# Pooled attention and a gelu MLP: another order at the start of the first product, and partial sums of group 0 kept in SBUF

## The chip, the cores and the metric

One core of a Trainium2 chip. The metric is the device time of one execution in microseconds (us); the median of 5 runs of the kernel before is 302.25 (302.09 to 302.32).

## What is computed

Attention with pooled keys and values, 8 batches of 8 heads, 576 queries, head size 64; then a two-layer MLP on its output as 4608 rows of 512:

```
k_p = k.reshape(B, H, 72, 8, D).mean(axis=3)          # 8 keys pooled into one; v the same
scores = q @ k_p^T / sqrt(D);  attn = softmax(scores)
x = (attn @ v_p) as (4608, 512)
h = x @ w_in                                          # 512 -> 2048
out = (0.5 * h * (1 + tanh(c * (h + 0.044715 h^3)))) @ w_out   # 2048 -> 512
```

## The kernel before

The work is one stream written out by hand in program order: each engine does its instructions in the order in which the code emits them, and waits come from the data. TensorE (PE) does all products, ScalarE (ACT) exponentials, logarithms and gelu, VectorE (DVE) the pooling, the multiplication by the inverse denominator and the eviction of results, GpSimd (POOL) issues most loads, SyncE (SP) the stores and the transposing DMAs.

**Batch 0** is done alone at the start (lines 425 to 481). Scores `qk` and `expo` for the halves c = 0, 1 of the queries and the pairs of heads pr = 0 to 3; `den0(c, pr, bank)` forms the denominators of two pairs at once, `inverse0` (L354 and L356 in the profile) their inverse as exp(-ln), `av0(c, pr, bank)` (L363) the weighted values, and `mult0` (L367) multiplies into xT, the transposed input of the MLP. `spin(n, bank)` (L421) is n matmuls of zeros whose result nobody reads. The values come through `v_steps(0)`, three adds on DVE (L150).

**Nine groups of 512 rows** follow, g = 0 to 8. Each has

- a first product, `p1_mm(g, fo, ko)` (L396): for each of 16 tiles fo of 128 hidden columns, four matmuls ko over the 512 inputs into the PSUM bank that `h_bank` names; ko is also the pair of heads that xT's rows come from, so ko 0 and 1 need `mult0` of pairs 0 and 1 only. `gelu` (L402) then writes gT.
- a second product, `p2_mm(g, r, fo, bank)` (L405): for each row tile r of 128 rows, 16 matmuls over fo into the bank that `o_bank` names (row tiles 0 and 2 share one bank, 1 and 3 the other); `store` evicts it on DVE (L410) and SP sends four DMAs (L415). The 64 matmuls are counted by m, and the attention of the next batch is hung in between by `at(m, f, ...)`.

Group 0's first product takes its first four tiles as ko 0, 1, and then ko 2, 3. During it DVE pools the keys of batch 1 (`k_steps`, L150) for the transposes `trans_k` after fo = 11 (L212). In its second product, `v_half(1, 0)` at m = 3 and `v_half(1, 1)` at m = 18 pool the values of batch 1, three DVE adds each, and the eight pieces of attention of batch 1 run at

```
pos = (6, 14, 20, 27, 34, 41, 48, 55, 61)
at(pos[i], qk, nb, *ORDER[i], 2)
a = (nb, *ORDER[i - 1], 4 + 2 * ((i - 1) % 2))
at(pos[i], av, *a)                      # bank 4 or 6, used by every second piece
at(min(pos[i] + 9, ...), mult, *a)      # DVE, L340
```

so `av` at m = 27 writes the bank that `mult` of m = 23 reads. Its second product takes rows 0 and 1 together, four fo at a time, then row 2, then row 3. Batch 2 and later use another way: the keys go through kz and a transposing DMA on SP to kx (L178), which `rem_scores` at m = 2 of the group before (L296) reads. Their loads are issued by `load_next`, held back for batch 2 by a copy `gate` on POOL (L506) until q of batch 2 has been transposed by DMA (L256).

**Loads.** q of batch 0, w_in (two halves along the input), k, part of v and q of batch 1, w_out (four quarters along the hidden size), and q of batch 2 are issued by POOL in this order on one queue; a DMA on it waits for the eighth before it. The first k and v come through SP and ACT; v of batch 1 (`load_v(1, [nc.sync])`) through SP, released by a one-column memset of its tile on DVE (L485).

Of the kernel before, what the change touches and what calls it, by code (L numbers as in the profile page):

```python
# [8 lines left out]
F32 = mybir.dt.float32  # L9
BF16 = mybir.dt.bfloat16  # L10
ALU = mybir.AluOpType
# [7 lines left out]
def kernel(  # L19
# [9 lines left out]
    nc = tc.nc  # L29
# [3 lines left out]
    DM = H * D  # L33
    DF = moe_w_in.shape[1]
    KO = DM // 128
    FO = DF // 128
    T = S // 32
    TP = T // 2
    CH = S // 2
# [11 lines left out]
    ep = ctx.enter_context(tc.tile_pool(name="ep", bufs=2))  # L51
    gpool = ctx.enter_context(tc.tile_pool(name="gp", bufs=1))
    opool = ctx.enter_context(tc.tile_pool(name="op", bufs=5))
# [4 lines left out]
    PS = psp.tile([128, 8, 512], F32, name="PS")  # L58
# [4 lines left out]
    vts = [consts.tile([128, 4, 512], F32, name=f"vt{i}") for i in range(2)]  # L63
# [23 lines left out]
    def load_v(b, engs):  # L87
        rows = v[b].rearrange("h (j l) d -> j h (l d)", l=8)
        for i in range(2):
            engs[i % len(engs)].dma_start(out=vts[b % 2][64 * i:64 * i + 64], in_=rows[0:64, 4 * i:4 * i + 4])  # L90
# [8 lines left out]
    w_in_b = [consts.tile([128, KO // 2, DF], BF16, name=f"w_in_b{i}") for i in range(2)]  # L99

    w_out_b = consts.tile([128, FO, DM], BF16, name="w_out_b")
    w_in_v = moe_w_in.rearrange("(ko p) f -> p ko f", p=128)
# [8 lines left out]
    make_identity(nc, identb)  # L111

    def load_w_in(i):
        nc.gpsimd.dma_start(out=w_in_b[i], in_=w_in_v[:, 2 * i:2 * i + 2])  # L114

    load_w_in(0)
    load_w_in(1)
    load_k(1, [nc.gpsimd])
    load_q(1)
# [157 lines left out]
    def window(w, h):  # L277

        c = h * 2 * D - h % 2 * D
        return w.rearrange("j h a d -> j (h a d)")[:, c:c + 128]  # L280
# [63 lines left out]
    def den0(c, pr, bank):  # L344
        for x in range(2):
            e = es[0, c, pr + x]
            for y in range(2):
                one = ones.rearrange("j a d -> j (a d)")[:, 64 - 64 * y:192 - 64 * y]
                nc.tensor.matmul(out=PS[:, bank + x, :CH], lhsT=one, rhs=e[:, y, :],
                                 start=(y == 0), stop=(y == 1))  # L350

    def inverse0(c, pr, bank):
        ld = ep.tile([128, 2, CH], F32, name="ld0", bufs=1)
        nc.scalar.activation(out=ld, in_=PS[:, bank:bank + 2, :CH], func=ACT.Ln)  # L354
        rc = ep.tile([128, 2, CH], F32, name="rc0")
        nc.scalar.activation(out=rc, in_=ld, func=ACT.Exp, scale=-1.0)  # L356
        rcs[0, c, pr] = rc

    def av0(c, pr, bank):
        for x in range(2):  # L360
            e = es.pop((0, c, pr + x))
            for y in range(2):
                nc.tensor.matmul(out=PS[:, bank + x, :CH], lhsT=window(vz, 2 * (pr + x) + y),  # L363
                                 rhs=e[:, y, :], start=(y == 0), stop=(y == 1))

    def mult0(c, pr, bank):
        nc.vector.tensor_tensor(out=xT[:, pr:pr + 2, c * CH:(c + 1) * CH], in0=PS[:, bank:bank + 2, :CH],  # L367
                                in1=rcs.pop((0, c, pr)), op=ALU.mult)
# [7 lines left out]
    def x_bank(g):  # L376
        return g % 2

    def h_bank(g, fo):
        x, y = x_bank(g), 1 - x_bank(g)  # L380
        if g == 0 and fo < 4:
            return 4 + fo
        if g and fo == 4:
            return 5
        return (x, 2, 3, y)[fo if fo < 4 else (fo - 1) % 4]

    def o_bank(g, r):
        return 1 - x_bank(g) if r % 2 == 0 else x_bank(g)

    gTs = {}  # L390

    def p1_mm(g, fo, ko):
        r0 = g * GROUP
        q, j = divmod(fo, 4)
        w = w_in_b[ko // 2][:, ko % 2, q * 512 + j:(q + 1) * 512:4]
        nc.tensor.matmul(out=PS[:, h_bank(g, fo), :], lhsT=w, rhs=xT[:, ko, r0:r0 + GROUP],  # L396
                         start=(ko == 0), stop=(ko == KO - 1))

    def gelu(g, fo):
        if g not in gTs:  # L400
            gTs[g] = gpool.tile([128, FO, GROUP], BF16, name="gT")
        nc.scalar.activation(out=gTs[g][:, fo, :], in_=PS[:, h_bank(g, fo), :], func=ACT.Gelu_apprx_tanh)  # L402

    def p2_mm(g, r, fo, bank, c0=0, c1=DM):
        nc.tensor.matmul(out=PS[:, bank, c0:c1], lhsT=gTs[g][:, fo, r * 128:(r + 1) * 128],  # L405
                         rhs=w_out_b[:, fo, c0:c1], start=(fo == 0), stop=(fo == FO - 1))

    def store(g, r, bank):
        osb = opool.tile([128, DM], F32, name="osb")
        nc.vector.tensor_copy(out=osb, in_=PS[:, bank])  # L410

        for n in range(4):
            b, col = divmod(g * GROUP + r * 128 + n * 32, S)
            rows = out[b * S:(b + 1) * S].rearrange("(p t e) d -> e t p d", t=TP, e=2)
            nc.sync.dma_start(out=rows[col // CH, col % CH // 32], in_=osb[n * 32:(n + 1) * 32])  # L415


    def spin(n, bank):

        for _ in range(n):  # L420
            nc.tensor.matmul(out=PS[:, bank, :], lhsT=idle[:, 0:128], rhs=idle, start=True, stop=True)  # L421
# [24 lines left out]
    for h in range(H):  # L446
        nc.tensor.matmul(out=PS[64:Sp, 7, h * D:(h + 1) * D], lhsT=identb[0:64, h:64:H],
                         rhs=kps[0][0:64, KR], start=True, stop=True)
    scores(1, 1, 0)
    den0(0, 0, 2)  # L450
    inverse0(0, 0, 2)
    nc.vector.tensor_copy(out=vz[64:Sp, :, 0], in_=PS[64:Sp, 7].rearrange("p (h d) -> p h d", d=D))
    trans_q(0, *QG[2], 5, nc.vector)
# [8 lines left out]
    for f in v_steps(0):  # L462
        f()
    inverse0(1, 0, 6)
    spin(2, 4)
    den0(0, 2, 2)
    inverse0(0, 2, 2)
    spin(2, 4)
    av0(0, 0, 4)
    mult0(0, 0, 4)  # L470
    den0(1, 2, 6)
    inverse0(1, 2, 6)
    av0(1, 0, 0)
    mult0(1, 0, 0)
    av0(0, 2, 4)
    mult0(0, 2, 4)
    spin(2, 0)
    av0(1, 2, 0)
    mult0(1, 2, 0)
    for t in kps:  # L480
        nc.vector.memset(t[:, KR + 1], 0.0)
    nc.vector.memset(kTs[1][0], 0.0)
    nc.vector.memset(kTs[1][1], 0.0)

    nc.vector.memset(vts[1][:, 0, 0:1], 0.0)  # L485
    load_v(1, [nc.sync])
    for w in vps:
        nc.vector.memset(w, 8.0)
    nc.gpsimd.memset(kz, 0.0)

    for fo, ko in [(fo, ko) for ko in range(2) for fo in range(4)]:
        p1_mm(0, fo, ko)


    for g in range(NG):
# [41 lines left out]
        if g + 1 == NG:  # L537
# [3 lines left out]
            for i, o in enumerate(gLs):  # L541
                side[4 * i + 3].append(lambda i=i, o=o: nc.vector.tensor_copy(  # L542
                    out=o.rearrange("p f (x t) -> p f t x", t=4),
                    in_=gTs[g][:, 4 * i:4 * i + 4, 384:].rearrange("p f (t x) -> p f t x", t=4)))
# [1 line left out]


        if g == 0:
            first = [(fo, ko) for ko in (2, 3) for fo in range(4)]
        else:  # L550
            late = 3
            rest = [fo for fo in range(4) if fo != late]
            first = [(fo, ko) for ko in range(3) for fo in rest]
            first += [(fo, ko) for fo in (late, 4) for ko in range(3)]
            first += [(fo, 3) for fo in rest + [late, 4]]
        for fo, ko in first:
            p1_mm(g, fo, ko)
        for fo in range(FO):
            if fo >= (5 if g else 4):
                for ko in range(KO):  # L560
                    p1_mm(g, fo, ko)
            gelu(g, fo)
            for s in side[fo]:
                s()
# [2 lines left out]
            load_next()  # L567


        todo = {}  # L570

        def at(m, f, *a):
            todo.setdefault(m, []).append((f, a))
# [41 lines left out]
        seq = [(r, fo) for r in range(4 if g + 1 < NG else 3) for fo in range(FO)]  # L615
        if g == 0:

            seq[:32] = [(r, 4 * f4 + f) for f4 in range(4) for r in range(2) for f in range(4)]
        for m, (r, fo) in enumerate(seq):
            for f, a in todo.pop(m, []):  # L620
                f(*a)
            p2_mm(g, r, fo, o_bank(g, r))
            if fo == FO - 1:
                store(g, r, o_bank(g, r))
        for m in sorted(todo):
            for f, a in todo[m]:
                f(*a)
    for c0, c1, bank in ((0, 384, o_bank(g, 3)), (384, DM, 4)):
        for fo in range(FO):
            nc.tensor.matmul(out=PS[:, bank, c0:c1], lhsT=gLs[fo // 4][:, fo % 4], rhs=w_out_b[:, fo, c0:c1],  # L630
                             start=(fo == 0), stop=(fo == FO - 1))
        osb = opool.tile([128, c1 - c0], F32, name="osb")
# [35 lines left out]
```

## Time and profile before

| | us |
|---|---|
| median of 5 runs | 302.25 |
| the profiled execution: its time | 302.49 |
| its span | 300.4 |
| PE busy | 291.5 (97%) |
| ACT busy | 216.6 (72%) |
| DVE busy | 152.8 (51%) |
| first product of group 0 starts | 21.30 |
| second product of group 0 starts | 36.43 |
| first product of group 1 starts | 54.67 |

Times are from the start of the span. In lines of a timeline the columns are start, length, engine, line of the kernel, operation, output<-input, shape and count; in brackets the idle time of the engine before it and what ended that. PEld is the loading of weights, which goes on beside matmuls. Neighbouring instructions of a kind are merged, and some matmul records are missing from a trace. A matmul of 128x512 is reported with 379 ns, but such matmuls start 0.2157 us apart.

### The profile page before, as it was taken

What the parts mean: (1) busy time and instruction counts of PE and PEld (TensorE: products, weight loads), DVE (VectorE), ACT (ScalarE), POOL (GpSimd) and SP (SyncE); (2) the same over time, 40 slices, a digit from 0 to 9 for tenths busy, and PEclk for the clock granted to TensorE, in tenths of its full rate; (3) what the DMA queues carried; (4) which work ended last, traced back from release to release, by engine and by line L of the source; (5) the groups of instructions that cost most, each with busy time, mean ns of one, the idle gap of its engine ahead of it and who ended that gap; (6) DMA issues with size and microseconds to landing.
All of it is one profiled execution on the core that took longest, in us unless ns stands there. A gap on an engine that the chain in (4) does not pass through costs nothing.

```text
span 300.4 us, 4347 instructions
## 1 busy us (share of the span) xinstructions
PE 291.5 (97%) x1498; PEld 151.0 (50%) x1527; DVE 152.8 (51%) x303; ACT 216.6 (72%) x408; POOL 37.4 (12%) x67
## 2 busy tenths in 40 slices
PE   8889999999999999999999999999999999999995
PEld 3555555554555455545554555455545555445443
DVE  4775587474576257716690659065924630111112
ACT  1686679879888897889878987798879887206500
POOL 7104001300600060006000410032000000000000
PEclk9999999999999999999999999999999999999999
DMA  7999986980799169835994498729961310121022
GB/s 227 270 252 262 251 168 131 241 196 13 177 262 185 33 160 249 178 74 130 237 208 85 97 258 201 103 54 255 232 119 36 75 37 0 37 70 36 0 69 73
DMA packets 38758, 43.11 MB, mean 144 GB/s; under 512 B 25488, under 2 KB 26128, under 8 KB 38608
## 3 DMA queue, kind: packets, MB, share of 16 engines
q0 software_dynamic: 8000, 24.39, 36.0%
q1 hardware_dynamic: 30032, 17.06, 25.2%
q10 hardware_dynamic: 704, 1.38, 1.3%
q8 instruction: 12, 0.20, 0.3%
q14 instruction: 10, 0.08, 0.1%
HBM read 36.70 MB, written 9.44 MB: 154 GB/s over the span
## 4 chain that ended last, share of the span: by engine, by line
PE 87%; DMA 7%; POOL 1%; DVE 1%; issue 1%; ACTq 0%; ACT 0%; DVEq 0%; POOLq 0%
PE PS L405 40%; PE PS L396 38%; DMA kt<-in_v_dram 7%; PE PS L322 4%; PE PS L311 2%; PE PS L630 1%; DVE kt L150 1%; PE PS L296 1%; PE PS L287 1%; PE PS L267 1%; POOL w_in_b L114 0%; POOL qb L95 0%; PE PS L236 0%; ACTq L183 0%; ACT gT L402 0%
## 5 line engine op out<-in xcount | busy, mean ns | idle before, releaser
L405 PE MATMUL PS<-w_out_b,gT 128*128 128x512 bf16 x543 | 134.5, 379 | 0.9 <-issue 0.2
L396 PE MATMUL PS<-xT,w_in_b 128*128 128x512 bf16 x565 | 125.7, 379 | 0.7
L402 ACT ACTIVATE gT<-PS 128x512 bf16<-128x512 f32 x144 | 79.2, 606 | 45.7 <-PE PS L396 45.7
L396 PEld LDWEIGHTS <-w_in_b 128*128 128x128 bf16 x576 | 65.0, 113 | 58.8 <-DMA w_in_b<-in_moe_w_in_dram 0.3
L405 PEld LDWEIGHTS <-gT 128*128 128x128 bf16 x560 | 53.8, 97 | 51.0 <-issue 1.7
L340 DVE TENSOR_TENSOR xT<-PS,rc 64x288 bf16<-64x288 f32 x112 | 51.0, 455 | 20.4 <-ACT rc L332 17.8
L410 DVE COPY osb<-PS 128x512 f32<-128x512 f32 x35 | 24.2, 692 | 50.2 <-PE PS L405 46.8
L317 ACT ACTIVATE eT<-PS 64x576 bf16<-64x576 f32 x48 | 30.7, 640 | 0.6
L304 DVE COPY eT<-er 8x576 bf16<-8x576 bf16 x24 | 7.3, 303 | 39.3 <-ACT er L302 38.8
L329 ACT ACTIVATE ld<-PS 64x288 f32<-64x288 f32 x56 | 22.5, 403 | 5.6 <-PE PS L322 5.1
L332 ACT ACTIVATE rc<-ld 128x288 f32<-128x288 f32 x56 | 24.8, 443 | 1.8
L373 ACT ACT_TABLE_LOAD x17 | 21.8, 1283 | 3.6 <-issue 3.3
L150 DVE TENSOR_TENSOR kt<-kt 128x1280 f32<-128x1280 f32 (+5 forms) x18 | 18.9, 1048 | 10.2 <-DMA kt<-in_v_dram 6.5
L330 ACT ACTIVATE ld<-PS 64x288 f32<-64x288 f32 x56 | 22.5, 403 | 1.4
L322 PE MATMUL PS<-eT,vp 72*128 72x288 bf16 x96 | 19.7, 285 | 0.1
L150 DVE TENSOR_TENSOR vt<-vt 128x1024 f32<-128x1024 f32 (+3 forms) x18 | 17.1, 952 | 1.8 <-DMA vt<-in_v_dram 1.5
L502 POOL COPY gate<-eT 1x2 bf16<-1x2 bf16 x5 | 0.9, 174 | 125.3 <-DMA eT<-er 125.3
L322 PEld LDWEIGHTS <-vp 72*128 72x128 bf16 x96 | 9.5, 98 | 11.3
L274 ACT ACTIVATE e<-PS 72x576 bf16<-72x576 f32 x16 | 9.9, 644 | 2.9 <-PE PS L267 2.6
L421 PE MATMUL PS<-idle 128*128 128x512 bf16 x32 | 9.5, 434 | 1.6 <-DVE idle L139 1.2
L311 PE MATMUL PS<-qT,kx 128*128 128x288 bf16 x48 | 9.8, 286 | 0.0
L542 DVE COPY kt<-gT 128x512 bf16<-128x512 bf16 x4 | 3.0, 745 | 11.6 <-ACT gT L402 11.6
(64 smaller groups left out, 128.4 us busy)
## 6 DMA issues: line engine op xcount, KB each, us to landing
out_dram<-osb SPq DMA_DIRECT2D x141, 64.0 KB
kt<-in_k_dram POOLq DMA_DIRECT2D x12, 512.0 KB, 6.8
vt<-in_v_dram POOLq DMA_DIRECT2D x12, 512.0 KB, 10.5
qb<-in_q_dram POOLq DMA_DIRECT2D x7, 576.0 KB, 14.9
w_in_b<-in_moe_w_in_dram POOLq DMA_DIRECT2D x2, 1024.0 KB, 16.7
w_out_b<-in_moe_w_out_dram POOLq DMA_DIRECT2D x4, 512.0 KB, 24.4
vt<-in_v_dram SPq DMA_DIRECT2D x3, 512.0 KB
kt<-in_k_dram POOLq DMA_DIRECT2D x1, 1024.0 KB, 22.4
```

The lines of the kernel that those rows point to most:

```text
L150: nc.vector.tensor_tensor(out=o, in0=a, in1=b, op=ALU.add)
L317: nc.scalar.activation(out=eT[0:64, 2 * pr:2 * pr + 2, c, :], in_=PS[64 * c:64 * c + 64, 2:4, :CH], func=ACT.Exp, scale=1.0 / 64.0)
L322: nc.tensor.matmul(out=PS[:, bank + x, :CH], lhsT=window(vps[b % 2], 2 * pr + x), rhs=eT[:, 2 * pr + x, c, :], start=True, stop=True)
L329: nc.scalar.activation(out=ld[0:64], in_=PS[64:128, bank, :CH], func=ACT.Ln)
L330: nc.scalar.activation(out=ld[64:128], in_=PS[0:64, bank + 1, :CH], func=ACT.Ln)
L332: nc.scalar.activation(out=rc, in_=ld, func=ACT.Exp, scale=-1.0)
L340: nc.vector.tensor_tensor(out=xT[rows, pr, col:col + CH], in0=PS[rows, bank + x, :CH], in1=rc[rows], op=ALU.mult)
L373: nc.scalar.preload_act_table_set(name)
L396: nc.tensor.matmul(out=PS[:, h_bank(g, fo), :], lhsT=w, rhs=xT[:, ko, r0:r0 + GROUP], start=(ko == 0), stop=(ko == KO - 1))
L402: nc.scalar.activation(out=gTs[g][:, fo, :], in_=PS[:, h_bank(g, fo), :], func=ACT.Gelu_apprx_tanh)
L405: nc.tensor.matmul(out=PS[:, bank, c0:c1], lhsT=gTs[g][:, fo, r * 128:(r + 1) * 128], rhs=w_out_b[:, fo, c0:c1], start=(fo == 0), stop=(fo ...
L410: nc.vector.tensor_copy(out=osb, in_=PS[:, bank])
```

## The change

- `load_w_in`: the first half of w_in comes as two DMAs, hidden columns 0 to 1023 and 1024 to 2047, so nine DMAs instead of eight stand ahead of w_out.
- Batch 0: `av0(1, 0)` goes ahead of `den0(1, 2)`, `av0(1, 2)` ahead of `av0(0, 2)` and into bank 2; the last filler `spin(2, 0)` is gone; rc0 has three buffers.
- The memset that releases `load_v(1)`, and that load, come ahead of the other memsets.
- First product of group 0: six tiles on ko 0 and 1, then the same six on ko 2 and 3, each tile's two matmuls together; other banks.
- Second product of group 0: all four row tiles on fo 0 to 7 (rows 0 and 1, then 2 and 3), then on fo 8 to 15 (rows 2 and 3, then 0 and 1). Rows 0 and 1 are copied to SBUF after fo = 7 (m = 11 and 15), and their second half is added to that copy in `store`.

```diff
     def load_w_in(i):
-        nc.gpsimd.dma_start(out=w_in_b[i], in_=w_in_v[:, 2 * i:2 * i + 2])
+        n = DF if i else DF // 2
+        for c in range(0, DF, n):
+            nc.gpsimd.dma_start(out=w_in_b[i][:, :, c:c + n], in_=w_in_v[:, 2 * i:2 * i + 2, c:c + n])
...
-        rc = ep.tile([128, 2, CH], F32, name="rc0")
+        rc = ep.tile([128, 2, CH], F32, name="rc0", bufs=3)
...
-        if g == 0 and fo < 4:
-            return 4 + fo
+        if g == 0 and fo < 8:
+            return (0, 1, 6, 7, 4, 5, 2, 3)[fo]
...
-    def store(g, r, bank):
-        osb = opool.tile([128, DM], F32, name="osb")
-        nc.vector.tensor_copy(out=osb, in_=PS[:, bank])
+    def store(g, r, bank, sums=None):
+        if sums is None:
+            osb = opool.tile([128, DM], F32, name="osb")
+            nc.vector.tensor_copy(out=osb, in_=PS[:, bank])
+        else:
+            osb = sums
+            nc.vector.tensor_tensor(out=osb, in0=PS[:, bank], in1=sums, op=ALU.add)
...
     mult0(0, 0, 4)
+    av0(1, 0, 0)
+    mult0(1, 0, 0)
     den0(1, 2, 6)
     inverse0(1, 2, 6)
-    av0(1, 0, 0)
-    mult0(1, 0, 0)
+    av0(1, 2, 2)
     av0(0, 2, 4)
     mult0(0, 2, 4)
-    spin(2, 0)
-    av0(1, 2, 0)
-    mult0(1, 2, 0)
+    mult0(1, 2, 2)
+
+    nc.vector.memset(vts[1][:, 0, 0:1], 0.0)
+    load_v(1, [nc.sync])
...
-    for fo, ko in [(fo, ko) for ko in range(2) for fo in range(4)]:
+    for fo, ko in [(fo, ko) for fo in range(6) for ko in range(2)]:
         p1_mm(0, fo, ko)
...
-            first = [(fo, ko) for ko in (2, 3) for fo in range(4)]
+            first = [(fo, ko) for fo in range(6) for ko in (2, 3)]
...
-            if fo >= (5 if g else 4):
+            if fo >= (5 if g else 6):
...
-            seq[:32] = [(r, 4 * f4 + f) for f4 in range(4) for r in range(2) for f in range(4)]
+            seq = [(r, 4 * (2 * i + f4) + f) for i in range(2) for rs in ((0, 1), (2, 3))[::1 - 2 * i]
+                   for f4 in range(2) for r in rs for f in range(4)]
...
-            p2_mm(g, r, fo, o_bank(g, r))
+            part = g == 0 and r < 2
+            p2_mm(g, r, fo, o_bank(g, r), last=7 if part and fo < 8 else FO - 1, first=8 if part and fo >= 8 else 0)
+            if part and fo == 7:
+                sums[r] = opool.tile([128, DM], F32, name="osb")
+                nc.vector.tensor_copy(out=sums[r], in_=PS[:, o_bank(g, r)])
             if fo == FO - 1:
-                store(g, r, o_bank(g, r))
+                store(g, r, o_bank(g, r), sums.get(r) if part else None)
```

More of the change, by code (lines that the diff above doesn't have):

```diff
@@ L402, in gelu, with p2_mm @@
         nc.scalar.activation(out=gTs[g][:, fo, :], in_=PS[:, h_bank(g, fo), :], func=ACT.Gelu_apprx_tanh)
-    def p2_mm(g, r, fo, bank, c0=0, c1=DM):
-        nc.tensor.matmul(out=PS[:, bank, c0:c1], lhsT=gTs[g][:, fo, r * 128:(r + 1) * 128],
-                         rhs=w_out_b[:, fo, c0:c1], start=(fo == 0), stop=(fo == FO - 1))
-    def store(g, r, bank):
-        osb = opool.tile([128, DM], F32, name="osb")
-        nc.vector.tensor_copy(out=osb, in_=PS[:, bank])
+    def p2_mm(g, r, fo, bank, first=0, last=FO - 1):
+        nc.tensor.matmul(out=PS[:, bank], lhsT=gTs[g][:, fo, r * 128:(r + 1) * 128],
+                         rhs=w_out_b[:, fo], start=(fo == first), stop=(fo == last))
+    def store(g, r, bank, sums=None):
[5 more added lines that the diff above has]
+            nc.vector.tensor_tensor(out=osb, in0=PS[:, bank], in1=sums, op=ALU.add)
         for n in range(4):
@@ L483 @@
     nc.vector.memset(kTs[1][1], 0.0)
-    nc.vector.memset(vts[1][:, 0, 0:1], 0.0)
-    load_v(1, [nc.sync])
     for w in vps:
@@ L567 @@
             load_next()
-        todo = {}
+        todo, sums = {}, {}
         def at(m, f, *a):
```

## Prediction, made before the changed kernel was run

> **What bounds the kernel now.** I read the busy shares first, then the table of stretches, then the timelines of VectorE and TensorE from 17 us to 70 us, and last the landings of the DMAs.
>
> ```profile
> PE 291.5 (97%) x1498; PEld 151.0 (50%) x1527; DVE 152.8 (51%) x303; ACT 216.6 (72%) x408; POOL 37.4 (12%) x67
> ```
> ```profile
> 17.80:21.30 3.50, 3.15 (x22) 2.17 (x23) 2.60 (x4) 2.73 (x5) 0.19 (x1) 1.00 1.08 231
> 21.30:31.67 10.37, 10.32 (x50) 5.37 (x49) 6.08 (x11) 5.87 (x11) 3.26 (x3) 1.00 1.05 278
> ...
> 36.43:54.67 18.24, 18.11 (x101) 9.82 (x101) 13.24 (x24) 15.81 (x32) 3.59 (x7) 1.00 0.77 161
> ```
>
> Each row of the second view gives a stretch, its length and the busy time of PE, PEld, DVE, ACT and POOL, then clock, DMA share and GB/s. A busy PE proves little by itself, so I checked starts: neighbouring 128x512 matmuls start 0.2157 us apart. From the first product at 21.30 to the first K transpose at 31.67 there are 48 of them, 48 x 0.2157 = 10.35 of the 10.37 us. After 21.3 us I find no gap in the starts except single missing records. So the time is (start of the first product) + (PE work) + (stalls), and the stalls are now about zero. The change removes no PE work after 21.3 us. It can gain only by starting earlier, at most until something else is late, and every new stall is paid in full.
>
> **Start of the first product: -1.0 us.** Before:
>
> ```profile
> 18.59 0.76 DVE L367 TENSOR_TENSOR xT<-PS,rc 128x576 bf16<-128x576 f32 x1 [0.38 <-PE PS L363]
> 19.57 1.42 DVE L367 TENSOR_TENSOR xT<-PS,rc 128x576 bf16<-128x576 f32 x2 [0.22 <-PE PS L363]
> ```
> ```profile
> 20.38 0.59 PE L421 MATMUL PS<-idle 128*128 128x512 bf16 x2 [0.33 <-DVE xT L367]
> ```
>
> The product needs the first two multiplications of batch 0. The second, now 19.57 to 20.28, waited for av0(1,0), which stood behind den0. The change puts av0(1,0) first, so its multiplication runs straight after the first, 19.37 to 20.08. On PE, five steps of four 288-column matmuls follow each other from 17.82, each 0.495 us by the starts (17.82, 18.32, 18.81): 17.82 + 5 x 0.495 = 20.30. The two filler matmuls (0.43 us) and the 0.33 us wait go. The third buffer of rc0 removes the wait of ACT at 19.45 (0.67 us <- DVE xT), so the last reciprocal ends near 20.9, and the last multiplication near 22.1; neither is on the path, because twelve matmuls of the first two head sets (2.59 us) now run until 22.89 instead of eight until 23.02. Their banks are free: fo 2 and 3 use banks 6 and 7, whose Ln should end at 20.2, and are due at 21.2; fo 4 and 5 use bank 4 and 5, multiplied by 21.3, due at 22.0.
>
> **w_in in three transfers.** The second half of w_in lands at 22.93 before (PEld waits for it 0.26 us at 22.97). Twelve matmuls are over at 22.89, so at best 0.1 us of wait stands here. The split doubles the packets of the first half. In the trace a packet that reads 8 KB takes 0.322 us, one that reads 4.6 KB 0.191; on that line a 4 KB one takes about 0.172 (estimate). 256 packets on 16 engines are 16 each: 16 x (2 x 0.172 - 0.322) = +0.35 us for everything behind on the queue. The rule that speaks against this is in the Trainium skill, DMA: Bandwidth & Descriptors, section Bandwidth: batch transfers to 1 MiB or more; its table (64 KB 0.95 us, 1 MB 6.15 us) puts two of 0.5 MB at 0.6 us over one of 1 MB. The queue is backlogged here, so set-up is hidden and the rule's end is high; I take 0.3, bounds 0 and 0.6. One more issue on POOL (0.7 us) costs nothing while the queue is full. It also shifts the ring of eight completion counts: qb of batch 1 is now issued behind the first qb's landing (8.57), the w_out parts behind one earlier landing each; all still wait in the backlog.
>
> **The K load of batch 1.** PE's next dependence is the K transpose:
>
> ```profile
> 27.88 2.35 DVE L150 TENSOR_TENSOR kt<-kt 128x1280 f32<-128x1280 f32 x2 [2.70 <-DMA kt<-in_v_dram]
> 30.27 0.49 DVE L150 TENSOR_TENSOR kp<-kt 128x320 bf16<-128x320 f32 x1
> 30.79 0.72 ACTq L183 DMA_DIRECT2D vp<-kp  x1
> 31.45 0.48 PEld L212 LDWEIGHTS <-kp 128*128 128x128 bf16 x5
> ```
>
> kp is ready at 30.76 and PE comes at 31.67: 0.9 us of slack, about what the change spends. kp hangs on a DMA (27.76), not on PE, so it does not come earlier. Later it can: +0.3 for the split, and the V load of batch 1 is released about 0.95 us earlier (its memset stood at 22.98, now right after the last multiplication). Its packets began at 27.31, 4.2 us after the first issue, and took 80 to 100 KB per us from a DMA total near 250; begun at 26.4 they take some of the K load's last 1.3 us, 0 to 0.5 us. So PE reaches the transpose between 30.9 (no shift) and 31.7 (all). The same shifts move the second quarter of w_out, which landed at 37.79 for use at 38.63 (m = 8 of the second product). I take a remaining gain of 0.3 us at the second product, bounds 0 and 0.8.
>
> **The second product of group 0: +1.2 us.** Here the change adds work to DVE:
>
> ```profile
> 37.63 1.93 DVE L150 TENSOR_TENSOR vt<-vt 64x1024 f32<-64x1024 f32 x2
> 39.59 0.42 DVE L150 TENSOR_TENSOR vp<-vt 64x256 bf16<-64x256 f32 x1
> 40.16 1.95 DVE L150 TENSOR_TENSOR vt<-vt 64x1024 f32<-64x1024 f32 x2 [0.15 <-DMA vt<-in_v_dram]
> 42.15 0.42 DVE L150 TENSOR_TENSOR vp<-vt 64x256 bf16<-64x256 f32 x1
> 42.60 0.94 DVE L340 TENSOR_TENSOR xT<-PS,rc 64x288 bf16<-64x288 f32 x2
> ```
> ```profile
> 43.96 0.41 PE L287 MATMUL PS<-e,vp 72*128 72x288 bf16 x2
> ```
>
> S is the start of the second product (36.43 before). The built order of DVE puts both copies of partial sums between the first and the second v_half. Each is a 128x512 eviction, 0.69 us by its row. The second waits for the matmul of m = 15, which starts at S + 4.20 and ends at S + 4.58: copy S + 4.62 to 5.31. The second v_half takes 2.41 (40.16 to 42.57), so it ends at S + 7.75 (before S + 6.14), and the first multiplication of batch 1 at S + 8.72 (before S + 7.11). av at m = 27 needs that v_half, and its second matmul the banks that this multiplication reads. It starts at S + 8.82; before, at S + 7.66 with 0.5 us to spare. So PE stands 1.2 us, with the whole rest of the stream behind it in order. This is counted from S, hence an earlier S doesn't shorten it. Its bounds are narrow (1.1 to 1.3), since all the rows are measured; only an earlier v_half would take it away, and V's landing (34.07 and 40.14) is not late.
>
> The other waits that the order adds fit. The first partial-sum copy ends at S + 4.29, its bank is due at S + 4.42; the second S + 5.31 against S + 5.78. Rows 2 and 3 end at m = 43 and 47; their evictions are 0.4 to 0.5 us ahead of m = 48 and 52. The two additions have no row: not below the copy's 0.69, and by the nearest one that reads PSUM and SBUF (288 columns 0.455) not over 0.8; I take 0.7. They replace two copies, and the next group's first bank is due 0.2 us after, so 0 to 0.1. w_out's last two quarters (40.55, 43.02) are now used at m = 32 and 40 instead of 16 and 24: this cover is real, but PE never waited for them before; with PE no earlier, it gains nothing.
>
> **Group 1's first key transposes.**
>
> ```profile
> 64.73 1.29 SPq L178 DMA_TRANSPOSE kx<-kz  x1
> ```
>
> kx lands at 68.79, PE uses it at 69.0, so this chain (qb landing 45.80, transposes, the gate, K loads from 51.25, DVE from 60.85) has 0.15 us of slack. It moves with the queue, +0.3, and the stores of rows 0 and 1 now come last: some 0.25 MB more lies beside the K loads at about 200 to 250 KB per us, 0 to 0.6 us. PE is 0.9 late by then, which covers most of it; I add 0.05, bounds 0 and 0.5.
>
> **The clock.** A TensorE that waits might be slowed. The granted clock is 1.00 in every stretch, and the longest wait now is 0.33 us, so no row shows one of 1.2 us. The Trainium skill, TensorE: Matmul & The Clock Gate, section What's actually happening, puts the fall to half rate after an idle window of about 3.4 us. By it the stall costs 1.2; if the clock fell for one such window, 3.4 x 0.5 = 1.7 us more (estimate). I take zero.
>
> **Sum.** +1.2 - 0.3 + 0.05 = +0.95 us. The profiled execution has a span of 300.4 and a time of 302.49; such an execution should then have a span of 301.35 and a time of 303.44. The median before is 302.25, 0.24 below that execution, so the median is forecast at 303.2. A difference of 0.2% (0.6 us) is what I call a change.
>
> **Rivals.** (a) DMA keeps its times: S gains 0.8, so +1.2 - 0.8 = +0.4, 302.65. For it: the backlog's bytes are the same. Against: packet times. Chance 0.2. (b) Everything late adds: no gain at S and kx late by 1.2 beyond its slack, +1.5, 303.75; the point is a kx landing past 70. Chance 0.2. (c) Faster: the evictions slip into DVE time that nobody needs. That happens if the first multiplication frees its bank before S + 7.66; it needs 1.2 us less DVE work ahead of it than the rows show. Then only the gain at S is left, -0.8 to -0.3, 301.45 to 301.95. Against it is the order of DVE. Chance 0.07. (d) As forecast, 0.53.
>
> **Range and chances.** From the bounds: low 302.6, high 303.9. Slower by over 0.2% is (b), (d) and a little of (a): 0.74. Within: most of (a) and part of (c), 0.2. Faster 0.06.
>
> **What would show it.** First product's start at 20.3; kp in 30.8 to 31.6 and PE waiting for it; two 0.69 us evictions between the v_halves near 40 to 41; a PE wait of about 1.2 us for a DVE multiplication before av, and its start near 44.8; group 1 beginning near 55.6. Wrong if av doesn't wait, if the product starts much before 20.3, or if PE waits for kx for over 0.5 us.

## The result and the profile after

| | before | after |
|---|---|---|
| median of all runs, us | 302.38 (71) | 303.03 (36) |
| ratio after/before, 95% interval | | 1.0031 (1.002 to 1.0041) |
| the profiled execution: time / span | 302.49 / 300.4 | 303.01 / 300.9 |
| first product of group 0 starts | 21.30 | 20.38 |
| second product of group 0 starts (S) | 36.43 | 36.14 |
| first product of group 1 starts | 54.67 | 55.23 |

The change makes the kernel slower by 0.31%, about 0.9 us; the medians differ by 0.65 us, the two profiled executions by 0.52. The single times after lie in two heaps: 20 from 302.27 to 303.17 (their median is 302.58), and 16 from 303.61 up (median 304.21). The granted clock averages 0.999 in both heaps, so the clock does not make the upper one; it is taken up below.

The start is as planned. VectorE's (DVE's) multiplications of batch 0, after:

```profile
18.69 1.42 DVE L370 TENSOR_TENSOR xT<-PS,rc 128x576 bf16<-128x576 f32 x2 [0.66 <-ACT rc L359]
20.65 1.61 DVE L370 TENSOR_TENSOR xT<-PS,rc 128x576 bf16<-128x576 f32 x2 [0.54 <-PE PS L366]
```

The first two are now one row, back to back, and the first product starts 0.92 us earlier. The table of stretches then shows where it goes (columns as before):

```profile
17.80:20.38 2.58, 2.58 (x22) 1.98 (x21) 1.66 (x3) 2.45 (x5) 0.53 (x1) 1.00 1.08 218
20.38:31.06 10.68, 10.50 (x49) 5.34 (x48) 6.83 (x12) 6.56 (x11) 3.26 (x3) 1.00 1.05 285
36.14:55.23 19.09, 18.19 (x101) 9.82 (x101) 14.52 (x26) 15.81 (x32) 3.87 (x7) 1.00 0.77 155
```

To the K transposes it is 10.68 us instead of 10.37 for the same 48 matmuls: TensorE (PE) waits for w_in's second half, which landed at 23.22. The weight load sits idle for 0.60 us until then, and the next matmul starts 0.29 us late:

```profile
23.26 0.80 PEld L399 LDWEIGHTS <-w_in_b 128*128 128x128 bf16 x5 [0.60 <-DMA w_in_b<-in_moe_w_in_dram]
```

The second product's stretch takes 19.09 instead of 18.24, with the same PE work and 1.28 us more on DVE. The granted clock is still 1.00.

In that stretch, DVE:

```profile
39.29 0.42 DVE L153 TENSOR_TENSOR vp<-vt 64x256 bf16<-64x256 f32 x1
39.63 0.68 DVE L634 COPY osb<-PS 128x512 f32<-128x512 f32 x1
40.75 0.69 DVE L634 COPY osb<-PS 128x512 f32<-128x512 f32 x1 [0.44 <-PE PS L408]
41.48 1.95 DVE L153 TENSOR_TENSOR vt<-vt 64x1024 f32<-64x1024 f32 x2
43.45 0.42 DVE L153 TENSOR_TENSOR vp<-vt 64x256 bf16<-64x256 f32 x1
43.91 1.92 DVE L343 TENSOR_TENSOR xT<-PS,rc 64x288 bf16<-64x288 f32 x4
```

and PE behind it:

```profile
43.42 0.41 PE L270 MATMUL PS<-qT,kT 128*72 128x288 bf16 x2
44.41 0.28 PE L290 MATMUL PS<-e,vp 72*128 72x288 bf16 x1 [0.58 <-DVE xT L343]
44.90 0.28 PE L290 MATMUL PS<-e,vp 72*128 72x288 bf16 x1 [0.21 <-DVE xT L343]
```

The two copies (L634) hold the second v_half back until 41.48, and both matmuls of av wait for the multiplication behind it. By starts the two waits are 0.74 and 0.37 us, 1.11 together. The order before had two smaller waits, behind the eviction of row 0:

```profile
44.63 0.69 DVE L410 COPY osb<-PS 128x512 f32<-128x512 f32 x1 [1.09 <-PE PS L405]
45.35 0.94 DVE L340 TENSOR_TENSOR xT<-PS,rc 64x288 bf16<-64x288 f32 x2
```

By starts, the first matmul of row 2 waited 0.08 us for that eviction (45.37, bank of row 0), and an av matmul waited 0.18 us (46.34) for the multiplication behind it. In the new order both are gone: 1.11 - 0.26 = 0.85 = 19.09 - 18.24.

The third place is one that the prediction passed over. After, from 29.9 us on, on ScalarE (ACT) and PE:

```profile
30.48 0.73 ACTq L186 DMA_DIRECT2D vp<-kp  x1
31.26 1.09 ACT L405 ACTIVATE gT<-PS 128x512 bf16<-128x512 f32 x2 [2.85 <-PE PS L399]
```
```profile
31.06 0.44 PE L215 MATMUL PS<-identb,kp 128*128 128x128 bf16 x5
31.91 0.38 PE L399 MATMUL PS<-xT,w_in_b 128*128 128x512 bf16 x1 [0.40 <-ACT gT L405]
```

The small DMA vp<-kp stands on ACT's queue after gelu of fo = 7 and waits there until DVE has written kp (30.45). Gelu of fo = 8 is behind it, and the matmul of fo = 12 needs the bank that this gelu reads. The bracket of the gelu names PE, but PE had long been done; it is the DMA ahead that kept it. The same is in the profile of before:

```profile
31.55 1.09 ACT L402 ACTIVATE gT<-PS 128x512 bf16<-128x512 f32 x2 [2.54 <-PE PS L396]
```
```profile
32.20 0.59 PE L396 MATMUL PS<-xT,w_in_b 128*128 128x512 bf16 x2
```

So PE's path had no slack at all toward the K load: the matmul of fo = 12 starts 1.45 us after kp in both.

### The profile page after: what moved, and what is told of

The parts are those of the page before. It is cut to its first block, busy times and chain, and to the rows that moved or that the text cites. A ratio compares the mean times of both kernels' runs of the same rounds, so it can differ in the third digit from the quotient of the medians.

```text
span 300.9 us, 4343 instructions
## 1 busy us (share of the span) xinstructions
PE 292.1 (97%) x1496; PEld 151.3 (50%) x1525; DVE 154.0 (51%) x305; ACT 216.5 (72%) x408; POOL 38.1 (13%) x68
## 4 chain that ended last, share of the span: by engine, by line
PE 89%; DMA 6%; ACT 1%; POOL 1%; issue 1%; DVE 0%; POOLq 0%
PE PS L399 40%; PE PS L408 39%; DMA w_in_b<-in_moe_w_in_dram 6%; PE PS L325 4%; PE PS L314 2%; PE PS L642 1%; PE PS L299 1%; PE PS L290 1%; PE PS L270 0%; POOL w_in_b L117 0%; POOL qb L95 0%; PE PS L239 0%; DVE xT L343 0%; ACT rc L335 0%; ACT ld L333 0%
## 5 line engine op out<-in xcount | busy, mean ns | idle before, releaser
L414 DVE COPY osb<-PS 128x512 f32<-128x512 f32 x33 | 22.8, 692 | 48.2 <-PE PS L408 44.8
L428 PE MATMUL PS<-idle 128*128 128x512 bf16 x30 | 10.3, 492 | 1.2 <-DVE idle L142 1.2
## 6 DMA issues: line engine op xcount, KB each, us to landing
vt<-in_v_dram POOLq DMA_DIRECT2D x12, 512.0 KB, 10.8
```

## Experiments

The first theory: the two copies on DVE cost 0.85 us net, and the start gives only what the K load lets through. Rivals: the split load of w_in and the early V load are the loss; the stores of rows 0 and 1, now last, delay kx and make the upper heap of times. Each comparison below is with the kernel before in the same series. The table has the places of every profiled execution, in us: K is the landing of the last part of batch 1's K load, kp the end of the pooling of these keys, fo 12 the start of that matmul, and stretch the time from S to group 1's first product.

| | K | kp | fo 12 | S | stretch | its time | median | ratio to before (95%) |
|---|---|---|---|---|---|---|---|---|
| before | 27.76 | 30.76 | 32.20 | 36.43 | 18.24 | 302.49 | 302.38 | |
| after | 27.46 | 30.45 | 31.91 | 36.14 | 19.09 | 303.01 | 303.03 | 1.0031 (1.002 to 1.0041) |
| a2 | 27.28 | 30.28 | 31.73 | 35.97 | 19.09 | 302.83 | 302.88 | 1.0031 (1.0012 to 1.005) |
| e1 | 28.41 | 31.41 | 32.86 | 37.09 | 18.24 | 302.98 | 301.65 | 0.9982 (0.9968 to 0.9996) |
| e2 | 27.08 | 30.08 | 31.75 | 35.99 | 19.09 | 302.62 | 302.87 | 1.0016 (1.0002 to 1.003) |
| e3 | 26.95 | 29.95 | 31.41 | 35.64 | 18.65 | 301.97 | 303.11 | 1.0016 (0.9999 to 1.0033) |
| f1 | 27.68 | 30.68 | 32.13 | 36.36 | 18.24 | 302.05 | 301.78 | 0.998 (0.9969 to 0.9991) |
| f2 | 27.61 | 30.61 | 30.95 | 35.19 | 19.36 | 301.99 | 301.79 | 0.9977 (0.997 to 0.9985) |
| f3 | 26.80 | 29.81 | 31.26 | 35.49 | 18.33 | 301.42 | 301.54 | 0.9972 (0.9964 to 0.9979) |
| f4 | 26.79 | 29.79 | 31.15 | 35.38 | 19.47 | 302.39 | 302.28 | 0.9987 (0.9968 to 1.0006) |
| g1 | 27.20 | 30.20 | 31.66 | 35.89 | 19.09 | 302.76 | 302.84 | 1.001 (0.9985 to 1.0035) |
| g2 | 27.01 | 30.01 | 30.95 | 35.18 | 20.24 | 302.91 | 303.38 | 1.0033 (1.0015 to 1.0051) |
| g3 | 27.88 | 30.87 | 32.32 | 36.55 | 19.82 | 304.19 | 304.19 | 1.0057 (1.0036 to 1.0078) |
| h1 | 27.55 | 30.55 | 31.99 | 36.22 | 19.10 | 303.20 | 303.15 | 1.0024 (1.0012 to 1.0036) |

Three things can be checked with it.

- From group 1's first product to the end of the last matmul it is 241.96 or 241.97 us in twelve of the fourteen traces (242.07 in e1, 242.11 in f3). So nearly all differences between these executions are made before S or in the stretch behind it.
- fo 12 follows kp by 1.44 to 1.46 us in every row whose key DMA is still ahead of gelu of fo = 8 on ACT, but for e2. In these rows S is K + 8.68 us, to 0.01, whatever the start of the first product.
- In e2, which has the old start, K landed at 27.08, and PE itself came 0.2 us too late for it (S is K + 8.91). So the new start pays only in executions in which K lands early enough, by e2's S before about 35.99 - 8.68 = 27.3 (an estimate).

### e1: the new start and loads alone

```diff
-            seq = [(r, 4 * (2 * i + f4) + f) for i in range(2) for rs in ((0, 1), (2, 3))[::1 - 2 * i]
-                   for f4 in range(2) for r in rs for f in range(4)]
+            seq[:32] = [(r, 4 * f4 + f) for f4 in range(4) for r in range(2) for f in range(4)]
...
-                store(g, r, o_bank(g, r), sums.get(r) if part else None)
+                store(g, r, o_bank(g, r))
```

> The changed kernel with the second product of group 0 as before (rows 0 and 1 on all of fo together, no sums in SBUF): only the new start and the new loads are left. Theory (DVE copies are the cost): no wait at av of m = 27, so the 0.3 us that the changed kernel has gained at the start of the second product stays, less what w_out or kx take: 0.1 to 0.3 us faster than before, and 0.9 us faster than the changed kernel. Rival (the loads and the split of w_in are the cost): as slow as the changed kernel, 0.7 to 0.9 us over before. Rival (w_out is late for the old order): waits at m = 16 and 24, and no gain over before.

Measured: 0.18% faster than before (0.65 us by the medians, where 0.1 to 0.3 were expected), 1.2 us below the changed kernel in the same series. The stretch is 18.24 again and w_out is never waited for. So the new start with the new loads is a gain, and without the new second product no loss is left; the rivals that blame the loads or w_out for the loss fall. The profiled execution of e1 was one of its late ones (302.98; 15 of the 22 single times lie under 302.0) and shows what made this one late. PE and ACT of e1:

```profile
31.47 0.45 PE L215 MATMUL PS<-identb,kp 128*128 128x128 bf16 x5 [0.40 <-DVE kp L153]
32.86 1.46 PE L399 MATMUL PS<-xT,w_in_b 128*128 128x512 bf16 x6 [0.94 <-ACT gT L405]
```
```profile
31.44 0.73 ACTq L186 DMA_DIRECT2D vp<-kp  x1
32.21 2.06 ACT L405 ACTIVATE gT<-PS 128x512 bf16<-128x512 f32 x4 [3.96 <-PE PS L215]
```

A load has 16 completion marks in the trace. K's last part had 15 of them by 26.52 and the last at 28.41. DVE, ACT's queue and PE followed one after the other. The gain itself is not in this trace, whose S is later than before's; no early execution of e1 was traced. That its early executions are those with an early K, which the old start could not use, fits the lowest times (301.18 in e1, 301.93 before in the same series) and the trace of f3 below (K 26.80, 301.42), but no run has the new start alone with all the old loads and the old second product.

### e2: the new second product alone

The kernel before, with the changed `p2_mm`, `store`, `seq` and `sums`, and nothing else of the change.

> The kernel before with the second product of group 0 in the new order, with the two sums in SBUF: start and loads as before. Theory: av of m = 27 waits 1.1 us for DVE, two waits of 0.26 us in sum that the old order has for its evictions go, so 0.85 us slower than before, about 303.1 to 303.3. Rival (loads): same as before. Rival (the stores of rows 0 and 1 that now come last delay kx): PE waits for kx in group 1, and the single times spread over more than 1 us.

Measured: 0.16% slower, 0.57 us by the medians, somewhat less than the 0.85 expected but inside its interval (0.06 to 0.9 us). The stretch of its trace is as long as that of the changed kernel:

```profile
35.99:55.08 19.09, 18.30 (x103) 9.83 (x101) 14.51 (x26) 15.80 (x32) 3.88 (x7) 1.00 0.75 159
```

PE did not wait for kx, and one of the 13 single times is above 303.1; the rival with the stores finds no support.

The two parts do not add up in the medians. In this series e1 is 0.65 us below before and e2 0.57 above, which would give about zero together; the whole change (a2) is 0.58 above. Part of this is the share of late times: 8 of 22 in a2 (above 304) and 7 of 22 in e1 (302.43 and up, 0.8 us or more over its median), but one of 13 in e2. A rest is not explained.

### e3: the copies on ACT

```diff
-                nc.vector.tensor_copy(out=sums[r], in_=PS[:, o_bank(g, r)])
+                nc.scalar.copy(out=sums[r], in_=PS[:, o_bank(g, r)])
```

> The changed kernel with the two partial sums copied to SBUF by ScalarE, not VectorE. Theory: the second v_half starts near 39.75 instead of 41.48 and the wait at av of m = 27 falls from 1.1 us to 0.1 or 0.2 (ScalarE's own chain loses up to 0.6); time 0.9 to 1.0 us below the changed kernel, 0.2 us below before. Rival (the loads, or the order of the stores): no change from the changed kernel, or a slowdown since ScalarE has the longer row in this stretch.

Measured: the mechanism moved as expected, the time did not. The second v_half starts at 39.24 and av waits no more, but the second copy comes behind ACT's exponential and logarithms, and row 3 waits for its bank at m = 20:

```profile
42.08 1.24 PE L408 MATMUL PS<-w_out_b,gT 128*128 128x512 bf16 x5 [0.50 <-ACT osb L634]
```

The stretch is 18.65: half of the loss is back on another engine. The profiled execution (301.97) is the fastest of its 22; the median is 303.11, with 14 of the times over 303, so the gain of 0.9 us that was expected is not there. With such a spread the run decides nothing about the median.

### a2: the changed kernel again

> The changed kernel itself, for a second trace and the spread of its single times (so far some near 302.5 and some near 304). All theories expect the same median within 0.3 us. If the loads vary, the trace shows another landing of w_in, k or kx and a wait of PE that follows it; if only DVE is the cost, the traces agree within 0.1 us.

Measured: the same ratio, the same waits at av (0.74 and 0.37) and the same stretch; S is 0.17 earlier with K 0.18 earlier. 8 of 22 single times are above 304.

### f1, f2, f3, f4: what the start could give

All are e1 with one edit more. f1: `load_v(1)` and its memset go back behind the other memsets. f3: `n = DF` in `load_w_in`. f2: the key DMA after gelu of fo = 12:

```diff
-                plan = {0: kk[:-1], 7: kk[-1:], 11: tk, 13: tq[:1], 14: tq[1:2], 15: tq[2:3]}
+                plan = {0: kk[:-1], 12: kk[-1:], 11: tk, 13: tq[:1], 14: tq[1:2], 15: tq[2:3]}
```

f4 is f1 and f2 together.

> As e1_start_only (old second product), with the V load of batch 1 released where it was before, behind the other memsets. Theory (the prediction's: V's packets delay the last part of the K load): the single times near 303 (K landed at 28.4 there, PE waited for kp and then for gelu) become rarer, median 0.1 to 0.3 us below e1_start_only. Rival (K's last packets are late on one DMA engine for another reason): the same share of times near 303 and the same median.

Measured: no better median. One of 14 single times is above 302.4 against 7 of 22 in e1, but they are as rare in f3, which keeps the early V load. The profiled K landed at 27.68. The early V load is not shown to delay K: over all traces K lands at 27.37 on average with the late V load (five) and at 27.40 with the early one (nine).

> As e1_start_only, with the small DMA of the pooled keys' rest (vp from kp) issued by ScalarE after gelu of fo = 12, not after fo = 7. Theory (that DMA stands on ScalarE's queue until kp is there, gelu of fo = 8 behind it, and the matmul of fo = 12 behind that): the wait of PE at fo = 12 is gone (0.34 us in the changed kernel, 1.1 in e1_start_only), 0.3 to 0.6 us faster than e1_start_only. Rival (the K transposes alone hold PE): no gain.

Measured: the half that was expected, and a new wait; in all no gain over e1 that is clear of the noise (0.9977 against 0.9982). fo 12 starts 0.34 us after kp, right behind the transposes, and S falls to 35.19. That is 1.17 us under f1, whose K landed at nearly the same time: ACT's queue was the gate.

```profile
30.66 0.45 PE L215 MATMUL PS<-identb,kp 128*128 128x128 bf16 x5
30.95 0.81 PE L399 MATMUL PS<-xT,w_in_b 128*128 128x512 bf16 x3
```

But:

```profile
40.05 0.41 PE L290 MATMUL PS<-e,vp 72*128 72x288 bf16 x2 [0.84 <-DMA vp<-kp]
```

The DMA of 8 KB, issued at 32.08, landed at 39.91 beside the loads; av of m = 14 waits for it, 1.12 us by starts, and the stretch grows to 19.36. Issued at 30.48 in the changed kernel it lands at 38.23, 1.6 us before av at 39.87.

> As e1_start_only, with the first half of w_in in one transfer again. Theory (the split costs 0.3 us on the queue): the second half of w_in lands 0.3 us earlier, and K too, so up to 0.3 us faster in median. Rival (packet size does not matter, or the wait only moves to kp): within 0.1 us.

Measured: 0.28% faster than before, 301.54, the fastest of all versions and faster than both kernels; one of 17 single times is above 301.9. Against e1 the ratio is 0.1% lower, about 0.3 us, but the intervals overlap, so a cost of the split is not shown by the times. In f3 PE waits 0.15 us for kx in group 1 (kx landed at 68.26, and PE uses it 14.48 us after group 1's start instead of 14.34): an earlier S would meet this next.

> f1 and f2 together: the new start, the old second product, the V load late and the key DMA after fo = 12. Theory: both gains, 0.4 to 0.8 us below e1_start_only, about 301.0, which would be 1.3 us below before. Rival (av of group 0 or kx take it): PE waits at av for the second v_half, which lands later with a late V load, or at kx, and the time stays at that of e1_start_only.

Measured: no gain, as the rival has it, but not at the wait that it named. The key DMA, issued at 32.27, landed at 40.22, and av of m = 14 waits for it as in f2, 1.23 us by starts; av of m = 27 does not wait for the late V load. Nothing is left of the earlier S.

```profile
40.35 0.41 PE L290 MATMUL PS<-e,vp 72*128 72x288 bf16 x2 [1.07 <-DMA vp<-kp]
```

### g1, g2, g3, h1

g1 is the changed kernel with `n = DF`. g2 is f3 with the key DMA on SyncE (SP):

```diff
-        (nc.scalar if b == 1 else nc.sync).dma_start(out=vps[b % 2][64:Sp, :, 0], in_=kps[b % 2][0:64, KR])
+        nc.sync.dma_start(out=vps[b % 2][64:Sp, :, 0], in_=kps[b % 2][0:64, KR])
```

> The changed kernel with the first half of w_in in one transfer. Theory (the split delays the second half of w_in and K, and makes the times near 304 frequent): few single times above 303.5 (they were 8 of 22 in a2_changed_again), median 302.3 to 302.6, so 0.3 to 0.5 us better than the changed kernel; the wait at av stays 1.1 us. Rival (the times near 304 come from the new second product): their share stays a third.

Measured: 302.84, above the 302.3 to 302.6 that were expected, and 4 of 13 times at 303.5 or above. The wait at av stays (0.74 and 0.37). The upper heap of the changed kernel is not made by the split alone.

> f3_start_one_w_in (new start, one transfer for w_in, old second product) with the small vp<-kp DMA of batch 1 issued by SyncE, so that gelu of fo = 8 waits for nothing. Theory: PE's wait at fo = 12 (0.34 us) goes, the second product starts 0.3 us earlier, but kx in group 1 lands where it did (68.3), so PE waits there 0.4 to 0.5 instead of 0.15 and the time is within 0.1 us of f3_start_one_w_in. Rival (kx follows): 0.3 us faster. Rival (the small DMA lands late behind V on that queue): PE waits at av of m = 14, as in f2_start_key_dma_later.

Measured: the last rival, and stronger than in f2. S is 35.18, but the small DMA stands behind the V load on its queue and lands at 40.79; av of m = 14 waits 2.0 us by starts.

```profile
40.92 0.41 PE L290 MATMUL PS<-e,vp 72*128 72x288 bf16 x2 [1.84 <-DMA vp<-kp]
```

> The changed kernel with the second partial sum copied twice, so VectorE does one more 128x512 eviction of 0.69 us ahead of the second v_half; the output is the same. Theory (PE waits for VectorE at av of m = 27, one for one): the stretch from the second product of group 0 to the first product of group 1 grows from 19.09 to 19.75 to 19.8 us, and the time by 0.6 to 0.7 us. Rival (the wait at av is set by something else, a landing or ScalarE): the stretch stays within 0.2 us.

```diff
                 nc.vector.tensor_copy(out=sums[r], in_=PS[:, o_bank(g, r)])
+                if r == 1:
+                    nc.vector.tensor_copy(out=sums[r], in_=PS[:, o_bank(g, r)])
```

Measured: one more copy of 0.69 us ahead of the second v_half,

```profile
41.17 0.69 DVE L634 COPY osb<-PS 128x512 f32<-128x512 f32 x1 [0.44 <-PE PS L408]
41.89 0.69 DVE L636 COPY osb<-PS 128x512 f32<-128x512 f32 x1
42.62 1.95 DVE L153 TENSOR_TENSOR vt<-vt 64x1024 f32<-64x1024 f32 x2
```

and the stretch grows from 19.09 to 19.82, by 0.73. The median rises by over 1 us against the changed kernel's in other series, more than the 0.6 to 0.7 expected; a late K may be a part of it. This trace (304.19) lies 0.9 us above the lowest times (303.28), and its K had 15 of 16 marks by 26.94 and the last at 27.88. In the stretch, DVE's queue ahead of av is paid one for one.

> The changed kernel with both loads as before: w_in's first half in one transfer and the V load of batch 1 behind the other memsets. What stays new is the order of the start and the second product. Theory (the late times come from K's last part landing late, which the new loads make more frequent): single times above 303.5 become rare (at most 1 in 10; they were 8 of 22 in a2_changed_again and 4 of 13 in g1_changed_one_w_in), median 302.5 to 302.9. Rival (the order of the start itself, or the second product, makes them): a quarter or more stay above 303.5.

Measured: 303.15, 0.24% slower than before and above the 302.5 to 302.9 that were expected; 2 of 13 times above 303.5, which is between the two expectations. With the old loads S is 36.22, much as before: PE starts 1.1 us earlier and gains 0.2, as K, at 27.55, lands 0.2 earlier. PE:

```profile
30.63 0.44 PE L215 MATMUL PS<-identb,kp 128*128 128x128 bf16 x5
31.99 1.89 PE L399 MATMUL PS<-xT,w_in_b 128*128 128x512 bf16 x7 [0.92 <-ACT gT L405]
```

## Why the prediction was right, and where its steps were not

It forecast 303.2, 0.95 us more than 302.25. Measured are 303.03, 0.65 us over the median before in the same series, and by the ratio 0.9 (0.6 to 1.2). The direction and the main cost are right for the reason given. That the number is so close is in part luck: the cause that it names makes 0.85 us, an earlier K takes part of this away, and the upper heap, which it did not foresee, puts some back. Step by step:

- **Start, -1.0.** 20.38 for 20.30: right.
- **Split of w_in, +0.3 on the queue.** In this pair the second half landed at 23.22 for 22.93, and PE's wait was 0.29 us. That the shift is just 0.29 is in part chance: over all traces the second half lands at 22.73 on average with one transfer for the first half (22.59 to 22.93, six traces) and at 22.91 with two (22.57 to 23.22, eight traces). The difference, 0.18, is smaller than the spread of either. The upper bound of 0.6 was an estimate, and the mean shift is far below it. The side remark on the ring had its sign wrong: the parts of w_out wait for one later landing each, and are issued at 11.99, 15.38, 17.87 and 23.50 instead of 8.86, 11.54, 17.46 and 23.22. It cost nothing, for all four still landed earlier than before.
- **The K load, "0.9 us of slack".** This failed. It compared kp with PE's own transposes and left out the line quoted right there, ACT's key DMA at 30.79: through it gelu of fo = 8 and the matmul of fo = 12 already waited for kp. Before fo = 12 there was a gap of 0.26 us beyond the usual spacing of the starts (31.89 to 32.20), which the reading "no gap in the starts except single missing records" passed over. The slack was zero, so in this pair the earlier start brought nothing by itself. f2, which moves that DMA, starts fo 12 right behind the transposes.
- **K lands 0.3 to 0.8 later.** Also wrong here: 27.46, 0.3 earlier. The remaining gain at S came out as forecast, 0.29 for 0.3, but by luck: K happened to land earlier, and the 0.92 us of PE were not partly spent on a later K. The early V load shows no effect on K's landing (27.40 on average with it, 27.37 without).
- **Second product, +1.2.** The waits are 1.11 us, for the reason given and at the place given: 0.74 us before the first matmul of av and 0.37 before the second (e1 has none of it, e2 has it alone, g3 has more of it). What was missed are 0.26 us of waits in the old order; "the stalls are now about zero" was too strong. The net cost is 0.85.
- **The additions.** 0.692 us each, as the copy; they delay nobody.
- **kx, +0.05.** No wait: PE uses kx 14.34 us after group 1's start, before and after, and kx landed at 68.47, 1.1 us ahead. The pooling of K for batch 2 even began 0.3 us earlier (60.55).
- **Clock.** The granted clock is 1.00 in every row shown, through the stall of 1.11 us, and in g2 around the longest wait, 2.0 us. This agrees with the idle window of about 3.4 us that the Trainium skill gives (TensorE: Matmul & The Clock Gate, What's actually happening); no wait here is long enough to show it. "The longest wait now is 0.33 us" overlooked 0.65 us for kp at 8.23 in the trace of before, also at clock 1.00.

The sum for the two executions is -0.29 + 0.85 = 0.56 us, against 0.55 by the end of the last matmul (297.19 for 296.64). What is not in it is the rest to the ratio's 0.9 us: the upper heap. Its cause stays open. A late last mark of K made the times of e1 late in one trace, and in g3 it goes with 0.9 us; by S = K + 8.68 a time of 304.21 would need a K at about 28.7 (an estimate), and e1 shows one at 28.41. But no execution near 304 of the changed kernel was traced. Why so many times of the changed kernel are late is not known either. The start with both new loads has late times by itself (7 of 22 in e1), and few with one of these loads as before (1 of 14 in f1, 1 of 17 in f3); with the new second product, g1 and h1 have 4 and 2 of 13 although one or both loads are as before there. That does not settle it.

## What to carry to other kernels

Here, with an engine that is busy 97% of the time, an earlier start was worth only what the next landing let through. Follow every queue that waits for such a landing, also a DMA issue that stands between two activations. Work added to a side engine costs nothing only if nobody further down waits for that engine's next instruction; here 1.4 us of copies that themselves delayed nobody came out as 1.1 us of TensorE at the next multiplication. Of a change with several parts measure each alone: the new start with one w_in transfer and the early V load (f3) is 0.28% faster than before, and the second product that came with it took more than that away.

## What was not expected of the hardware

- DVE's wait for a load ends with the last of its 16 completion marks, and that one can be far behind the others. The last K part had 15 marks by 26.52 us and the sixteenth at 28.41 in e1; in e2 these were 27.02 and 27.08. In e1 this difference of nearly two microseconds held up the whole chain behind it.
- The DMA of 8 KB from SBUF to SBUF took 7.5 to 10.8 us while the profile gives the DMA engines a busy share of 1.06 to 1.07: issued at 30.48 it landed at 38.23 (changed kernel, ACT), at 32.08 it landed at 39.91 (f2, ACT), at 30.04 at 40.79 (g2, SP).
